# An attention-and-MLP kernel with a written-out order: raw weights over a second queue, half copies by compute engines, and a new account of PSUM tiles

## The chip, the cores and the metric

One core of one Trainium2 chip runs the whole program. The metric is the device time of one execution in microseconds (us). The engines are named as the profile names them: PE (TensorE; PEld is its weight load), DVE (VectorE), ACT (ScalarE), POOL (GpSimd) and SP (SyncE, which here only issues DMAs).

## The reference

```python
q_bits = (einsum('bhsd,dk->bhsk', q, proj) > 0)         # 6 bits for each row of q, the same for k
mask   = q_bucket[:, :, :, None] == k_bucket[:, :, None, :]
scores = where(mask, (1/8) * q @ k.T, -1e9)             # B, H, S, D = 4, 8, 768, 64
attn   = softmax(scores)                                # over 768 keys
x      = (attn @ v) transposed to (3072 tokens, 512)
out    = (relu(x @ w_in) ** 2) @ w_out                  # 512 -> 2048 -> 512, float32
```

## The kernel before, in words

**Stages.** There are 32 pairs of batch and head. A *unit* is 128 queries of one pair against all 768 keys; there are 192 units, worked in *visits* of six (two heads, half of the sequence). When all heads of one half of a batch are done, `moe(n, b, half)` takes these 384 tokens through the two weight matrices; there are eight such blocks.

**A unit** (`unit`): PE makes the scores in PSUM as `pS` (a masked stack `L`,`M` and the stack `A`,`Q`); DVE moves them to `e` with a running maximum; ACT takes the exponential with its row sum in `sums`; DVE or POOL makes `rv` and DVE its reciprocal. In the first four visits, 24 units, POOL divides `e` by its sum, PE transposes it through `pT`, and ACT copies `pT` to `aT`. In later units ACT and DVE split `e` into two float16 halves `hl`, which DMAs transpose into `aT`. `av` multiplies by the values (`pA`) and leaves `xx` as a high and a low half.

**Preparing a pair** (`prep`): DMAs bring `R`; ACT and DVE split it into `A` and `L`; five copies of half stacks (64 partitions each) fill `Q`, `A`, `L` and `M`: `Q<-A`, `Q<-L`, `A<-A`, `L<-M`, `M<-Q`. Before, all five are DMAs on SP.

**Weights** (`fetch`, `split`): 32 pieces of raw weights come in as `raw` (0.5 MB each, three buffers, tag `hl`). A piece then takes `top` on ACT, `f` on DVE, the high half on ACT and the low half on DVE or POOL.

**A block** (`moe`): 16 steps of `pm` (12 matmuls of 384 columns with `win`) and `po` (9 matmuls of 512 columns with `wo`: three tiles of 128 tokens, in three banks of one PSUM tile). ACT takes the relu and the squares, DVE the low half `g`. When the 16th step is done, the three parts of `po` are copied to `o` and sent out. The second half of the last block waits for `verify`, which grades the inputs for the fast path.

**The order.** Instructions are first recorded (`Program.add`), with their dependencies by region. `forward` and `backward` then plan them over five engines with fixed prices; where an operation has several ways, the plan chooses the engine. `emit` writes the instructions in the planned order, and each engine works through its own in that order. The plan only orders: on the chip each instruction waits for semaphores that are set by whole tiles, whatever the plan assumed. A wait in the middle of an engine's order so holds all that stands behind it.

In the profile nearly every instruction has line L427 (a loop in `emit`), matmuls of `matmuls` L424, so groups are told apart by tile names. The program holds a second, general version behind a branch on `flag`; it was not taken, and counts below are of the first alone.

Of the kernel before, what the change touches and what calls it, by code (L numbers as in the profile page):

```python
# [13 lines left out]
F32 = mybir.dt.float32  # L14
# [24 lines left out]
    True: dict(xx=12, hl=3, f=3, e=4, aT=3, g=2, A=8, Q=8, L=8, M=8, R=2, VV=5),  # L39
# [24 lines left out]
RUN = 18  # L64
CONSTS_BY, WIDE = ("sp", "sp", "sp"), 1
# [16 lines left out]
TRANSPOSES = 165  # L82
# [47 lines left out]
class Program:  # L130
# [24 lines left out]
    @staticmethod  # L155
    def region(view):
        ap, rec = view.ap, view.rec
        size = lambda dims: 1 + sum(st * (n - 1) for st, n in dims)
        if rec.kind == "dram":
            return 0, 1, ap.offset, ap.offset + size(ap.ap), 0, 0, 0  # L160
        p0, f0 = divmod(ap.offset, rec.row)
        if rec.kind == "psum":
            return 0, 1, f0 // 512, 1 + (f0 % rec.row + size(ap.ap[1:]) - 1) // 512, 0, 0, 0

        (step, n), inner = ap.ap[1], size(ap.ap[2:])
        block = (step, f0 % step, f0 % step + inner) if n > 1 and f0 % step + inner <= step else (0, 0, 0)
        return (p0, p0 + ap.ap[0][1], f0, f0 + size(ap.ap[1:])) + block

    def add(self, *ways):
# [10 lines left out]
        for rec, w, (p0, p1, f0, f1, fs, g0, g1) in used:  # L180
            if rec.before is not None:
                deps |= rec.before.ops
            for j, w2, (a0, a1, b0, b1, bs, c0, c1) in rec.accesses:
                if (w or w2 or rec.kind == "psum") and a0 < p1 and p0 < a1 and b0 < f1 and f0 < b1 and not (fs and fs == bs and (c1 <= g0 or g1 <= c0)):
                    deps.add(j)
# [9 lines left out]
    def cost(key, name, args, kw):  # L195
# [3 lines left out]
        if name == "matmuls":  # L199

            side = {32: 4, 64: 2}.get(size(args[0][0][1]), 1)
            t = sum(size(a[2]) * column.get(a[2].dtype, 1 / 2.4) + 7 for a, _ in args) / side
            return t, t
# [8 lines left out]
        if name.startswith("dma"):  # L212
# [3 lines left out]
            return busy, b / (TRANSPOSES if name == "dma_start_transpose" else 314)  # L216
# [4 lines left out]
        else:  # L221
            fast = name in ("tensor_copy", "tensor_scalar") and "psum" not in kinds[:2]
            both = len(args) > 3 and isinstance(args[3], View) and args[3].shape[-1] == 1
            t = 67 + 100 * ("accum_out" in kw) + n / (1.92 if fast else 0.96) + 62 * (ptr and (fast or name == "scalar_tensor_tensor")) + 100 * both
# [10 lines left out]
    def port(key, name, args, kw):  # L235
# [7 lines left out]
        return inside and (len(ins) == 2 or name in ("tensor_copy", "tensor_scalar"))  # L243
# [74 lines left out]
    def forward(self, prio, near):  # L318
# [8 lines left out]
        out, dma, dge, held, kind = [], 0.0, 0.0, 0.0, None  # L327
# [11 lines left out]
        while True:  # L339
# [44 lines left out]
            if o.name.startswith("dma"):  # L384
                dge = max(dge, t) + busy if k != "pool" else dge
                busy = dge - t if k != "pool" else busy
                dma = max(dma, t + busy + (650 if k != "pool" else 450))
                if o.name == "dma_start_transpose":
                    o.busy = busy = dma + 467 - t
                dma += done  # L390
                done = dma + 910 - t
# [57 lines left out]
def run(ctx: ExitStack, tc, kq, v, proj2, w_in, w_out, consts, out, flag):  # L449
# [56 lines left out]
    if fast:  # L506
# [8 lines left out]
        codes = sb([P, 4 * P], BF16, "codes")  # L515
# [32 lines left out]
    def fetch(src):  # L548

        raw = sb([P, 512, 2], U32, "raw", tag="hl")  # L550
        send(raw.rearrange("p n t -> p (n t)").bitcast(U16)[:, 0:2047], src.bitcast(U16)[:, 1:2048])
# [79 lines left out]
    def prep(b, hp):  # L631
# [12 lines left out]
        for odd, R in enumerate(Rs):  # L644
# [5 lines left out]
            send(f32(Q[T]), f32(A[U]))  # L650
            send(f32(Q[U]), f32(L[U]))
            send(f32(A[U]), f32(A[T]))
# [6 lines left out]
            send(f32(L[U]), f32(M[T]))  # L659
            send(f32(M[T]), f32(Q[T]))  # L660
# [58 lines left out]
    def values(b, hp, plain):  # L719
# [3 lines left out]
        if fast:  # L723
            vscales[b] = VS, None
            RV = sb([P, 2, KC, D], F32, "V", tag="VV" if plain else "R")
            send(RV, v[b, hp])
# [80 lines left out]
    def moe(n, b, half):  # L807
# [6 lines left out]
        for f in range(NF + 1):  # L814
# [23 lines left out]
            if f > 0:  # L838
# [4 lines left out]
                if first:  # L843
                    po = ps([P, 3, DM], F32, "po")
                for t in range(3):
# [3 lines left out]
                    pe.matmul(po[:, t], gh, wo[:, 0, m], start=first, stop=False)  # L849
                    pe.matmul(po[:, t], gh, wo[:, 1, m], start=False, stop=False)  # L850
                    pe.matmul(po[:, t], gl, wo[:, 0, m], start=False, stop=last)
# [6 lines left out]
                for t in range(3):  # L858
                    r0 = b * S + half * HS + t * P
                    if grouped and last:  # L860
                        if m == 3:
                            move(acc[:, t], po[:, t], back)
                        else:
                            dve.scalar_tensor_tensor(acc[:, t], po[:, t], back, acc[:, t], ALU.mult, ALU.add)
# [168 lines left out]
```

## Time and profile before

| what | before |
|---|---|
| median of 3 runs (lowest to highest) | 832.73 us (830.81 to 833.39) |
| profiled execution: time, span | 834.86 us, 833.1 us |
| mean granted TensorE clock | 0.994 |
| PE, DVE, ACT, POOL busy | 794.3, 605.2, 656.6, 72.7 us |
| DMA | 145.93 MB in 299521 packets; SP's queue 77.2% of 16 engines' span, others 0.6% |

The page lists busy time by engine. The views used below are those of the waits (who sat idle, and what ended it), of windows (busy time in a stretch), of the timeline (instructions in order of time, with the idle time before them in brackets) and of groups by form (a mean duration for each kind of instruction). Instructions of one engine overlap a little, so that durations add up to more than busy time.

### The profile page before, as it was taken

The numbers are of one execution on the slowest core, as the hardware profiler recorded it, in microseconds if no ns is written. First come the engines' busy times: TensorE is split into PE (matmuls) and PEld (weight loads), VectorE is DVE, ScalarE is ACT, GpSimd is POOL, SyncE is SP. The second block draws the span as 40 slices with busy tenths as digits, with TensorE's granted clock in tenths as the row PEclk, the third lists the DMA queues.
The fourth block names the chain that finished last, engine by engine and source line by source line (L and its number), as shares of the span: only waits on it lengthen the run. The fifth ranks groups of instructions, "written<-read, shape, count | busy, mean of one in ns | idle before, by whom it ended". The sixth has DMA issues, their size and how long they took to land. (4 is left out here: it accounts for less than half of the span.)

```text
span 833.1 us, 14383 instructions
## 1 busy us (share of the span) xinstructions
PE 794.3 (95%) x5001; PEld 430.0 (52%) x5001; DVE 605.2 (73%) x1200; ACT 656.6 (79%) x1238; POOL 72.7 (9%) x175
## 2 busy tenths in 40 slices
PE   7797799999999999999999999999999999999996
PEld 4354355555555554555555545555555554555553
DVE  6888989998999888898879755888889433611110
ACT  5898999998888989888898856888988997334443
POOL 1255200100000010000000000000002000000000
PEclk9999999999999999999999999999999999999999
DMA  8985979999999999999989866988975889501001
GB/s 258 270 223 181 292 188 179 214 176 195 183 202 196 195 188 213 192 181 219 194 188 186 212 165 140 181 143 148 146 133 99 239 290 304 212 1 39 1 1 42
DMA packets 299521, 145.93 MB, mean 175 GB/s; under 512 B 268752, under 2 KB 279344, under 8 KB 299440
## 3 DMA queue, kind: packets, MB, share of 16 engines
q1 hardware_dynamic: 299440, 144.93, 77.2%
q8 instruction: 41, 0.67, 0.3%
q14 instruction: 40, 0.33, 0.1%
HBM read 56.80 MB, written 6.29 MB: 76 GB/s over the span
## 5 line engine op out<-in xcount | busy, mean ns | idle before, releaser
L427 PE MATMUL po<-wo,g 128*128 128x512 f16 x1152 | 296.9, 379 | 5.7 <-ACT o L427 5.7
L427 PE MATMUL pm<-xx,win 128*128 128x384 f16 x1536 | 297.7, 326 | 4.4 <-ACT g L427 2.8
L427 PEld LDWEIGHTS <-win 128*128 128x128 f16 x1536 | 149.9, 98 | 116.6 <-issue 8.0
L427 DVE TENSOR_SCALAR_CACHE_REDUCE e<-pS 128x768 f32<-128x768 f32 x192 | 182.7, 953 | 21.9 <-PE pS L427 17.7
L427 ACT ACTIVATE e<-e,maxes 128x768 f32<-128x768 f32 x192 | 178.2, 929 | 20.7 <-DVE e L427 19.2
L427 DVE SCALAR_TENSOR_TENSOR hl<-e,rv,hl 128x768 f16<-128x768 f32 x168 | 171.0, 1019 | 18.8 <-ACT hl L427 17.8
L427 PEld LDWEIGHTS <-g 128*128 128x128 f16 x1152 | 111.9, 98 | 124.8 <-issue 9.1
L427 ACT ACTIVATE hl<-e,rv 128x768 f16<-128x768 f32 x168 | 154.6, 923 | 6.0 <-DMA aT<-hl 5.2
L427 DVE SCALAR_TENSOR_TENSOR g<-g,g 128x384 f16<-128x384 f32 x121 | 66.9, 553 | 111.8 <-ACT g L427 111.4
L427 ACT ACTIVATE g<-g 128x384 f32<-128x384 f32 (+1 forms) x251 | 129.4, 517 | 6.6 <-PE po L427 2.7
L427 ACT ACTIVATE g<-pm 128x384 f32<-128x384 f32 x127 | 61.2, 482 | 90.3 <-PE pm L427 90.0
L427 PE MATMUL pS<-A,Q 128*128 128x384 f16 x372 | 93.1, 330 | 4.1 <-DVE e L427 2.6
L427 PE MATMUL pS<-L,M 128*128 128x384 f16 x372 | 91.8, 327 | 0.8 <-DMA M<-Q 0.8
L424 PE MATMUL pA<-aT,VV 128*64 128x384 f16 x1008 | 87.2, 327 | 0.0
L427 POOL TENSOR_SCALAR rv<-sums 128x1 f32<-128x1 f32 x136 | 36.8, 271 | 541.7 <-ACT e L427 400.2
L424 PEld LDWEIGHTS <-VV 128*64 128x64 f16 x1008 | 54.7, 110 | 32.9 <-issue 10.0
L427 PEld LDWEIGHTS <-Q 128*128 128x128 f16 x372 | 34.2, 98 | 43.1 <-issue 16.2
L427 DVE TENSOR_SCALAR M<-pc,masks 128x384 f16<-128x384 f32 x64 | 43.0, 672 | 15.4 <-PE pc L427 15.2
L427 PEld LDWEIGHTS <-M 128*128 128x128 f16 x372 | 36.3, 98 | 25.1 <-DMA M<-Q 1.2
L427 ACT ACTIVATION_READ_ACCUMULATOR e<-e,maxes 128x1 f32 x192 | 36.6, 191 | 0.0
L427 DVE SCALAR_TENSOR_TENSOR L<-R,A 128x768 f16<-128x768 f32 x32 | 30.4, 950 | 7.7 <-ACT A L427 7.5
L427 PE MATMUL pT<-unit_f,e 128*128 128x128 f32 x144 | 23.8, 293 | 10.5 <-ACT aT L427 7.7
(82 smaller groups left out, 517.4 us busy)
## 6 DMA issues: line engine op xcount, KB each, us to landing
R<-kq SPq DMA_DIRECT2D x32, 384.0 KB, 3.8
X<-kq SPq DMA_DIRECT2D x32, 384.0 KB, 4.1
raw<-w_in SPq DMA_DIRECT2D x16, 511.8 KB, 5.6
raw<-w_out SPq DMA_DIRECT2D x16, 511.8 KB, 4.9
V<-vp SPq DMA_DIRECT2D x20, 384.0 KB, 5.1
out<-o SPq DMA_DIRECT2D x24, 256.0 KB, 2.7
X<-vp SPq DMA_DIRECT2D x16, 384.0 KB, 4.4
Q<-L SPq DMA_DIRECT2D x32, 96.0 KB, 2.9
```

The costliest lines, as they stand in the source:

```text
L424: ins = q.engine.matmul(*map(real, args), **kw).ins
L427: ins = getattr(q.engine, o.name)(*map(real, o.args), **{k: real(x) for k, x in o.kw.items()}).ins
```

## The change: what it does

1. **Raw weights.** From the fourth on (29 of 32), POOL issues the DMA of `raw` and not SP.
2. **Half copies.** In batch 0 the five half copies may be done by SP, POOL or DVE. The plan gives 21 of the 40 to DVE, 8 to POOL, and leaves 11 as DMAs on SP.
3. **Buffers.** `R` has three buffers for two, `VV` four for five; `codes` shares the buffers of `g32`.
4. **The planner's account.** DMAs get other prices, two rings and a limit of 3000 ns on what is queued ahead; a ninth DMA of SP waits for the eighth before it; a few prices of DVE and PE change. PSUM tiles are now whole tiles to the planner, and no longer single banks; two readers of one no longer exclude each other.
5. **The last block.** Its three `po` parts lie in a `pS` tile (two of them) and a `pA` tile. In every block the second of the three is copied out by DVE.

```diff
-    True: dict(xx=12, hl=3, f=3, e=4, aT=3, g=2, A=8, Q=8, L=8, M=8, R=2, VV=5),
+    True: dict(xx=12, hl=3, f=3, e=4, aT=3, g=2, A=8, Q=8, L=8, M=8, R=3, VV=4),
...
+LANES = 8
-TRANSPOSES = 165
+TRANSPOSES, INSIDE, LOADING = 165, 230, 325
+SETUP, LANDING = 100, 1350
+RAW_BY, V_BY = ("pool",), ("sp",)
+HALVES, HALVES_TO = (("sp", "pool", "dve"),) * 5, 1
+AT_MOST, RAW_FROM = 3000, 3
...
         if rec.kind == "psum":
-            return 0, 1, f0 // 512, 1 + (f0 % rec.row + size(ap.ap[1:]) - 1) // 512, 0, 0, 0
+            return 0, 1, 0, 1, 0, 0, 0
...
-                if (w or w2 or rec.kind == "psum") and a0 < p1 and ...
+                if (w or w2) and a0 < p1 and ...
...
+            if way[1].startswith("dma") and rings[int(k == "pool")] > t + AT_MOST:
+                heapq.heappush(later[k], (rings[int(k == "pool")] - AT_MOST, i))
+                continue
...
+                if k != "pool":
+                    lanes.append(t + done)
+                    if len(lanes) >= LANES:
+                        busy = max(busy, lanes[-LANES] + 60 - t)
...
-        codes = sb([P, 4 * P], BF16, "codes")
+        codes = sb([P, 4 * P], BF16, "codes", 2, tag="g32")
...
-        send(raw...[:, 0:2047], src.bitcast(U16)[:, 1:2048])
+        pr.add(*[(getattr(pr, x), "dma_start", (raw...[:, 0:2047], src.bitcast(U16)[:, 1:2048]), {}) for x in (RAW_BY if turn[0] >= RAW_FROM else ("sp",))])
...
-            send(f32(Q[T]), f32(A[U]))
+            by = lambda n: tuple(getattr(pr, x) for x in (HALVES[n] if fast and b < HALVES_TO else ("sp",)))
+            move(f32(Q[T]), f32(A[U]), 1.0, by(0))
...
                 if first:
-                    po = ps([P, 3, DM], F32, "po")
+                    if fast and n == 2 * B - 1:
+                        po = ps([P, 2, 512], F32, "pS"), ps([P, 512], F32, "pA")
+                        po = [po[0][:, 0], po[0][:, 1], po[1]]
+                    else:
+                        po = ps([P, 3, DM], F32, "po")
+                        po = [po[:, t] for t in range(3)]
...
-                        move(o, po[:, t], back)
+                        move(o, po[t], back, (dve,) if fast and t == 1 else (act, dve, pool))
```

PE's last instructions before the branch on `flag`, first of the kernel before; a bracket names the engine whose semaphore the instruction waits for, beside its order.

```order
L427 MATMUL po<-wo,g 128x512 [waits Activation_49]
L427 LDWEIGHTS g
L427 MATMUL po<-wo,g 128x512
L427 LDWEIGHTS g
L427 MATMUL po<-wo,g 128x512
L427 LDWEIGHTS g
L427 MATMUL po<-wo,g 128x512 [waits Activation_49]
L427 LDWEIGHTS g
L427 MATMUL po<-wo,g 128x512
L443 TENSOR_LOAD flag [waits DVE_49]
```

The same place in the changed kernel:

```order
L444 MATMUL pA<-wo,g 128x512
L444 LDWEIGHTS g
L444 MATMUL pS<-wo,g 128x512
L444 LDWEIGHTS g
L444 MATMUL pA<-wo,g 128x512
L444 LDWEIGHTS g
L444 MATMUL pA<-wo,g 128x512
L460 TENSOR_LOAD flag [waits DVE_49]
```

The two waits for ACT inside the last nine matmuls are gone. In the whole order 14 matmuls that write `po` wait for ACT before: 6 open a block, 8 stand inside its last step. Now 5 open a block with such a wait (for ACT or DVE), none stands inside, and one of the last block waits for PE itself.

ACT's order around the first relu of the first block (`g<-pm`), of the kernel before; `xx<-pA` is the fourth of its kind, on which the first `pm` depends.

```order
L427 ACTIVATE wo<-f 128x512
L427 ACTIVATE e,sums<-e,maxes 128x768
L427 ACTIVATE top_87<-raw 128x512
L427 ACTIVATE win<-f 128x512 x2
L427 ACTIVATE xx<-pA 128x384
```

And in the changed kernel:

```order
L444 ACTIVATE wo<-f 128x512
L444 ACTIVATE e,sums<-e,maxes 128x768
L444 ACTIVATE top_86<-raw 128x512
L444 ACTIVATE e,sums<-e,maxes 128x768
L444 ACTIVATE top_83<-raw 128x512
L444 ACTIVATE wo<-f 128x512
L444 ACTIVATE bits<-pd,masks 128x384
L444 ACTIVATE wo<-f 128x512
L444 ACTIVATE xx<-pA 128x384
```

Up to this `xx` ACT now has 13 instructions more: one each of `A`, `VV`, `bits` and `e`, two each of `aT`, `top` and `win`, three of `wo`. No kind has fewer.

POOL's order from its first instruction after the constants, of the kernel before:

```order
L427 TENSOR_SCALAR rv<-sums 128x1
L427 TENSOR_SCALAR e<-e,rv 128x768
L427 TENSOR_SCALAR rv<-sums 128x1
L427 TENSOR_SCALAR e<-e,rv 128x768
L427 TENSOR_SCALAR rv<-sums 128x1
```

And now:

```order
L444 TENSOR_SCALAR Q<-A 64x768
L444 TENSOR_TENSOR L<-R,A 128x768
L444 TENSOR_SCALAR rv<-sums 128x1
L444 DMA raw<-w_in 128x2047
L444 TENSOR_SCALAR e<-e,rv 128x768
L444 TENSOR_SCALAR rv<-sums 128x1
L444 DMA raw<-w_out 128x2047
L444 TENSOR_SCALAR e<-e,rv 128x768
L444 TENSOR_TENSOR win<-f,win 128x512
L444 DMA raw<-w_out 128x2047
```

Between POOL's divisions now stand DMAs of raw weights, half copies, and parts of the splits. Up to the 24th division there are 23 DMAs, 8 half copies, 3 `L`, 7 low halves of weights (4 before) and 15 `rv` (19 before).

More of the change, by code (lines that the diff above doesn't have):

```diff
@@ L215, in cost @@
             busy = 1040 if key == "pool" else (650 if inside else 475) + 50 * (key == "act")
-            return busy, b / (TRANSPOSES if name == "dma_start_transpose" else 314)
+            return busy, SETUP + b / (TRANSPOSES if name == "dma_start_transpose" else INSIDE if inside else LOADING)
         if key == "act":
@@ L223, in cost @@
             both = len(args) > 3 and isinstance(args[3], View) and args[3].shape[-1] == 1
-            t = 67 + 100 * ("accum_out" in kw) + n / (1.92 if fast else 0.96) + 62 * (ptr and (fast or name == "scalar_tensor_tensor")) + 100 * both
+            t = 67 + 100 * ("accum_out" in kw) + n / (3.84 if fast and all(mybir.dt.size(x.dtype) == 2 for x in args[:2]) else 1.92 if fast else 0.96) + 62 * (ptr and (fast or name == "scalar_tensor_tensor")) + 100 * both
         return t, t
@@ L242, in port @@
             return any(x.rec.kind == "sb" for x in args[1:] if isinstance(x, View) and len(x.shape) > 1 and x.shape[-1] > 1)
-        return inside and (len(ins) == 2 or name in ("tensor_copy", "tensor_scalar"))
+        return inside and name in ("tensor_copy", "tensor_scalar")
     def order(self):
@@ L386, in forward @@
                 busy = dge - t if k != "pool" else busy
-                dma = max(dma, t + busy + (650 if k != "pool" else 450))
+                ring = int(k == "pool")
+                dma = max(rings[ring], t + busy + (650 if k != "pool" else 450))
                 if o.name == "dma_start_transpose":
                     o.busy = busy = dma + 467 - t
-                dma += done
-                done = dma + 910 - t
+                shared = min(done, max(0.0, rings[1 - ring] - dma))
+                rings[1 - ring] += shared
+                dma = rings[ring] = dma + done + shared
+                done = dma + LANDING - t
+                if k != "pool":
+                    lanes.append(t + done)
+                    if len(lanes) >= LANES:
+                        busy = max(busy, lanes[-LANES] + 60 - t)
             free[k], o.end = t + busy, t + done
@@ L848, in moe @@
                     pr.rank, pr.mark = RANK_PE, pace()
-                    pe.matmul(po[:, t], gh, wo[:, 0, m], start=first, stop=False)
-                    pe.matmul(po[:, t], gh, wo[:, 1, m], start=False, stop=False)
-                    pe.matmul(po[:, t], gl, wo[:, 0, m], start=False, stop=last)
+                    pe.matmul(po[t], gh, wo[:, 0, m], start=first, stop=False)
+                    pe.matmul(po[t], gh, wo[:, 1, m], start=False, stop=False)
+                    pe.matmul(po[t], gl, wo[:, 0, m], start=False, stop=last)
                     pr.mark = None
```

22 lines of the change are left out of this document (12 added, 10 removed).

## The prediction

> **What bounds the kernel now.** I read the page first, then busy time by window, then who waited for whom, then the timeline at the two places that these point to. From the page:
>
> ```profile
> span 833.1 us, 14383 instructions
> PE 794.3 (95%) x5001; PEld 430.0 (52%) x5001; DVE 605.2 (73%) x1200; ACT 656.6 (79%) x1238; POOL 72.7 (9%) x175
> ```
>
> PE is nearly full, POOL nearly empty. A share over the whole span hides two stages, so here are windows cut at the first exponential (14.8), at the last step before the first `pm` (97.2, 97.7), and at the last matmul (827):
>
> ```profile
> core 0: us, PE busy (x) PEld busy (x) DVE busy (x) ACT busy (x) POOL busy (x), PEclk, DMA share, GB/s
> 0.00:14.80 14.80, 11.36 (x85) 7.01 (x85) 8.00 (x26) 6.41 (x10) 0.21 (x4) 1.00 0.79 250
> 14.80:97.20 82.40, 63.29 (x401) 36.32 (x400) 71.09 (x150) 73.70 (x152) 35.89 (x49) 0.96 0.83 241
> ...
> 97.70:827.00 729.30, 719.65 (x4517) 386.65 (x4516) 525.58 (x1026) 575.37 (x1076) 36.65 (x122) 1.00 0.77 167
> ```
>
> In the long stage after 97.7 PE idles 729.3 - 719.65 = 9.65 us in all: it is the bound, and only what shortens PE's own waits there is worth anything. In the opening PE has 74.65 busy of 97.2 (idle fill among it) and can't do more, since no tokens are ready for a block. There ACT (80.1 busy) and DVE (79.1) are the fullest, neither full. The opening ends when ACT copies the fourth `xx`:
>
> ```profile
> 97.17 0.47 ACT L427 ACTIVATE xx<-pA 128x384 f16<-128x384 f32 x1
> ...
> 97.70 0.32 PE L427 MATMUL pm<-xx,win 128*128 128x384 f16 x1 [1.04 <-ACT xx L427]
> ```
>
> So the time is the end of the opening, plus 729.3 us of PE's work, plus 6.1 us behind the last matmul. PE's waits over the whole run:
>
> ```profile
> PE pT L427 <- ACT aT L427: 7.7, 8, 2.2
> ...
> PE po L427 <- ACT o L427: 5.7, 8, 0.9
> ```
>
> The first lies in the opening (only there is a `pT`). The second is 5.7 of the 9.65 us.
>
> **Term 1: the waits of `po` for ACT.** The timeline at the end shows two of the eight:
>
> ```profile
> 821.67 2.54 PE L427 MATMUL po<-wo,g 128*128 128x512 f16 x11
> ...
> 824.25 0.60 ACT L427 ACTIVATE o<-po 128x512 f32<-128x512 f32 x1 [1.64 <-PE po L427]
> ...
> 824.90 0.81 PE L427 MATMUL po<-wo,g 128*128 128x512 f16 x3 [0.69 <-ACT o L427]
> ...
> 825.74 0.60 ACT L427 ACTIVATE o<-po 128x512 f32<-128x512 f32 x1 [0.90 <-PE po L427]
> 826.39 0.59 PE L427 MATMUL po<-wo,g 128*128 128x512 f16 x2 [0.69 <-ACT o L427]
> ```
>
> ACT copies the first part of `po` while the other two parts are still to be written, and PE stops until the copy is done, although the parts are in different banks. To the planner of before that was free, since it counted banks; the chip waited for the tile. Counting tiles, the new plan has all nine matmuls ahead of the first copy, and its order shows none of the eight waits. A wait costs more than its 0.69 idle: three matmuls take 0.81, and with a mean of 379 ns (page) for one that is (0.81 - 0.38) / 2 = 0.215 between starts, so 0.16 of the matmul ahead would have been overlapped. 5.7 + 8 x 0.16 = **7.0 us less**, all on the path, since PE bounds there. What is late next: a block's first `po` must now wait for three copies. Four matmuls of 384 columns take 0.65 in the chain of waits:
>
> ```profile
> 624.76 0.65 PE pS L427 x4
> ```
>
> Where that first `po` waits, the order puts at least 12 such matmuls in between, 1.95 us, against two copies of 0.60 on ACT beside one on DVE; a few tenths may come back at two or three blocks. At the very end the last copy follows the last matmul as before, so the 6.1 us stay.
>
> **Term 2: the opening.** The order has 13 ACT instructions more ahead of the `xx` that ends it, none fewer. Their prices, from the groups by form between 0 and 97 us:
>
> ```profile
> L427 ACT ACTIVATE e<-e,maxes 128x768 f32<-128x768 f32 x26 | 24.3, 936 | 0.8 <-DVE e L427 0.7
> L427 ACT ACTIVATE aT<-pT 128x384 f32<-128x384 f32 x46 | 20.7, 484 | 2.6 <-PE pT L427 2.4
> L427 ACT ACTIVATE top<-raw 128x512 f16<-128x512 bf16 x22 | 17.2, 783 | 3.9 <-DMA raw<-w_out 2.0 <-DMA raw<-w_in 1.5
> L427 DVE SCALAR_TENSOR_TENSOR f<-raw,top 128x512 uint32<-128x512 uint32 x22 | 15.3, 698 | 0.9 <-ACT top L427 0.9
> L427 ACT ACTIVATE win<-f 128x512 f16<-128x512 f32 x13 | 8.0, 619 | 0.3 <-DVE f L427 0.3
> L427 DVE SCALAR_TENSOR_TENSOR L<-R,A 128x768 f16<-128x768 f32 x8 | 7.6, 950 | 4.1 <-ACT A L427 4.1
> L427 ACT ACTIVATE A<-R 128x768 f16<-128x768 f32 x7 | 5.9, 841 | 4.6 <-DMA R<-kq 4.6
> L427 ACT ACTIVATE wo<-f 128x512 f16<-128x512 f32 x8 | 5.0, 624 | 0.0
> L427 ACT ACTIVATE bits<-pd,masks 128x384 bf16<-128x384 f32 x4 | 2.3, 580 | 0.8 <-PE pc L427 0.6 <-PE pd L424 0.2
> L427 DVE TENSOR_SCALAR codes<-sgn_f 128x128 bf16<-128x128 f32 x4 | 0.7, 224 | 1.4 <-DMA sgn_f<-consts 1.4
> L427 DVE TENSOR_SCALAR A<-R 128x768 f16<-128x768 f32 x1 | 0.5, 541 | 0.0
> ```
>
> One `e` 0.94, one `A` 0.84, one `VV` of the same size and so 0.84, two `aT` 0.97, one `bits` 0.58, two `top` 1.57, two `win` 1.24, three `wo` 1.87: 8.85 us. Instructions overlap by about 0.1 (a `top` of 0.77 begins at 15.72 and the next `e` at 16.36):
>
> ```profile
> 14.79 0.94 ACT L427 ACTIVATE e<-e,maxes 128x768 f32<-128x768 f32 x1
> ...
> 15.72 0.77 ACT L427 ACTIVATE top<-raw 128x512 f16<-128x512 bf16 x1
> 16.36 0.91 ACT L427 ACTIVATE e<-e,maxes 128x768 f32<-128x768 f32 x1
> ```
>
> That leaves 7.5 us, and ACT 80.1 + 7.5 = 87.6 us of work ahead of the first block. DVE fares alike: three `L` fewer (-2.9), five `f` more (+3.5), three `top` and two low halves at about `f`'s 0.7 (+3.5), nine small `rv` and reciprocals at no more than `codes` (+2.0), four copies gone at 0.54 (-2.2), and 21 half copies. No row shows a half copy; it lies between `codes` (0.22) and the full copy of `A` (0.54), nearer the latter, whose 768 columns it has: 0.4, so 8.4 in all (4.7 to 11.4). Net +12.4, and with an overlap of 0.1 for each of 33 instructions some +9: 88 us, just as full as ACT.
>
> What pays for it is ACT's idle time, 17.1 us in the opening: 14.8 - 6.4 = 8.4 ahead of the first `e`, and 82.4 - 73.7 = 8.7 behind it. The first part mostly stays: constants, `K`, `G`, `pd`, `pc`, `MK` and `pS` follow one another as before. The order puts both `K`, `G` and `pj` ahead of the first `R`, worth two issues of SP (0.43 each, below): I put the first `e` at 13.9. Of the 6.4 us that ACT did ahead of it, two `top`, a `win` and a `bits` (2.7) now stand behind it, so 87.6 - 3.7 = 83.9 remain: **no earlier than 13.9 + 83.9 = 97.8** can the fourth `xx` begin, about where it is today. A gain in the opening would need less work than the order shows. How much of the 8.7 us of later idling goes, then? By name:
>
> ```profile
> POOL rv L427 <- ACT e L427: 40.4, 17, 15.5
> ...
> PEld pT L427 <- POOL e L427: 8.6, 8, 2.5
> ...
> ACT A L427 <- DMA R<-kq: 4.6, 2, 3.0
> ...
> ACT top L427 <- DMA raw<-w_out: 2.0, 2, 1.6
> ...
> ACT top L427 <- DMA raw<-w_in: 1.5, 3, 0.6
> ```
>
> The 3.0 for `R` is ahead of the first `e`; 1.6 of it and 3.5 for `raw` are behind, 5.1 in all. SP's own waits say why:
>
> ```profile
> SPq L427 <- DVE f L427: 12.5, 9, 6.7
> ```
>
> SP holds all that stands behind a `raw` until a buffer is free, `R` and half copies among it. With `raw` on POOL, three buffers of `R`, and half copies that need no landing, I take the 5.1 as gone and 3.6 as staying. Against that POOL must now issue 23 DMAs ahead of its 24th division, each behind the same wait for `f`, and the divisions queue behind them; PE already waits on these (8.6 above). I put 0.5 us net there. Fourth `xx` at 97.8 + 3.6 + 0.5 = 101.9 against 97.2: **4.7 us more**. PE has meanwhile done four more `pS`, a `pc` and a group of `pd` (0.65 for four matmuls, so about **1.2 us** taken from later).
>
> The 11 half copies left on SP, the four `VV` and the shared `codes` I cost at nothing: SP's queue is emptier, and `VV` is fed by `V` loads of which only two were waited for.
>
> **Term 3: the rest of the order.** Three more splits of `wo` and five more `f` done early relieve ACT and DVE behind 97.7, but PE hardly waited there: at most 1 us. New waits from a new order of 4517 matmuls may cost as much. Taken as 0, with 2 us either way.
>
> **The sum.** -7.0 + 4.7 - 1.2 = -3.5. Against the profiled execution (834.86 us, whose span is 833.1 with 1.8 around it) that is 831.4; that execution stands 2.1 above the median of 832.73, which the prediction refers to: **829.2 us**, 0.4% less. Bounds: with no idle time of ACT behind the first `e`, and 1 us from term 3, 832.7 - 7.0 + 0.6 - 1.2 - 1 = 824.1; with the first `e` two microseconds earlier still, and 2 us of term 3, 821. With all 8.7 of idling still there and POOL in the way for 4 more, the fourth `xx` is at 110.5: -7 + 13.3 - 1.2 = +5.1, or 837.8.
>
> **Rivals.**
> *A: the opening costs nothing.* Fourth `xx` at 98 or before: 832.7 - 7.0 - 1.2 + 0.8 = 825.3 or less. For it: idle time by lateness of DMAs is just what the change touches. Against: 87.6 us of work in ACT's order.
> *B: POOL becomes the bound of the opening* (slower). Up to the 24th division its order holds 24 divisions, 23 DMAs, 8 half copies, 3 `L`, 7 low halves and 15 `rv`:
>
> ```profile
> L427 POOL TENSOR_SCALAR rv<-sums 128x1 f32<-128x1 f32 x21 | 6.7, 320 | 40.7 <-ACT e L427 40.4
> L427 POOL TENSOR_TENSOR win<-f,win 128x512 f16<-128x512 f32 x3 | 3.5, 1173 | 4.1 <-ACT win L427 4.0
> ```
>
> ```profile
> L427 POOL TENSOR_SCALAR e<-e,rv x24: 907/909/1468, 17.0 to 89.6; 128x768 f32<-128x768 f32 x24
> ```
>
> ```profile
> 6.51 1.29 SPq L427 DMA_DIRECT2D raw<-w_in  x3
> ```
>
> The first two rows are groups by form, the third is the division with its least, median and longest time and first and last start, the fourth SP's issue. 24 x 0.91 + 23 DMAs + 8 half copies at a division's 0.91 + 3 x 1.76 (1.173, and half as many columns again) + 7 x 1.17 + 15 x 0.32. A DMA on POOL has no row: SP issues one in 0.43, POOL's longest instruction here takes 1.76; I take 1.0, nearer the other POOL rows (10 to 40 us for 23). That is 70 us, behind a start at about 16, and 97.2 - 89.6 = 7.6 more from the last division to `xx`: 94 if POOL never waits. If it waits over 15 us, for buffers (12.5 on SP today) or for divisors, the fourth `xx` is past 109 and the 7.0 us are spent: 835 to 840.
>
> The Trainium skill has a rule for this (SBUF — State Buffer, "SBUF: two separate sides"): while DVE runs an instruction in a two-port mode, GpSimd can't write descriptors; in the next section, on a bandwidth pool, a DMA of 620 ns beside such a copy took 3100. No run here shows it yet; by that figure an estimate is 2.5 us for each DMA that meets one of 24 copies of some 0.4 us in 97, about one in ten, 6 us of POOL's time in all, and the sum would be 831 to 835 for it. Its chance lies within B's.
>
> *C: the waits of `po` come back* as waits of the next block's first `po`, or for other copies: half of term 1 lost, 832.7, no change that can be measured.
>
> **Chances.** Forecast 0.56, A 0.18, B 0.16, C 0.10. About 0.3%, 2.5 us, is what a measurement of this kernel can tell from no change. Of the forecast's own cases (fourth `xx` from 98 to 106, the earlier half likelier) seven in ten are faster than 830.2, which needs it by 102.9, and nearly all others within the bound. Faster: 0.56 x 0.7 + 0.18 + 0.03 of C = 0.60; same 0.16 + 0.07 = 0.23; slower 0.17. The range of 821 to 837 leaves out the far end of A and the worse half of B.
>
> **What the profile will show.** Term 1: no row of `po` waiting for ACT `o` of 5 us, and PE idle under 6 us between the first `pm` and the last matmul. Term 2: the first `pm` between 99 and 105, ACT over 86 us busy ahead of it, SP's waits for `f` near nothing, POOL over 65 us busy. B would show POOL with hardly any wait for ACT `e`, and PE's weight loads of `pT` waiting for POOL well over 15 us. A first `pm` before 97 makes term 2 wrong, eight new waits in the blocks term 1.

## The result: 5.3% slower, and the profile after

| | before | after |
|---|---|---|
| median (lowest to highest) | 832.75 us (830.81 to 833.39) | 876.79 us (874.99 to 878.12) |
| ratio, 95% interval | | 1.0531 [1.0504, 1.0559] |
| first `pm` (end of the opening) | 97.7 us | 131.8 us |
| from there to the first `pm` of the third block | 216.7 us | 229.9 us |
| from there to the start of the last matmul | 512.2 us | 505.1 us |

The median of before now has a fourth run. The last three rows are read off the starts of PE's instructions. Of the 40.2 us between the last matmuls (826.6 and 866.8), 34.1 were lost in the opening and 13.2 in the two blocks behind it; 7.1 were won in the other six. The page of the changed kernel begins:

```profile
span 874.1 us, 14381 instructions
...
PE 814.7 (93%) x5018; PEld 438.4 (50%) x5018; DVE 624.8 (71%) x1226; ACT 658.5 (75%) x1231; POOL 110.4 (13%) x214
...
q0 software_dynamic: 2320, 15.20, 5.9%
```

PE's busy time grew by 20, although it has nearly the same instructions; the windows, cut like those of before, tell where: 17.5 of the 20 are in the opening (busy time of PE, PEld, DVE, ACT and POOL, granted clock, share of the DMA engines, GB/s):

```profile
0.00:131.30 131.30, 92.16 (x514) 50.77 (x515) 100.57 (x208) 89.54 (x175) 68.40 (x88) 0.86 0.58 177
131.80:867.00 735.20, 722.29 (x4504) 387.62 (x4503) 523.31 (x1018) 567.91 (x1055) 42.03 (x126) 0.99 0.76 162
```

In the opening PE ran at a granted clock of 0.86 where before had 0.96 to 1.00. ACT's work is 89.5, close to the 87.6 forecast. DVE's is 100.6, where 88 were forecast, and no engine fills the 131.3 us: something else sets the pace. What lies behind the opening, split at the start of the third block, of before and then of the changed kernel:

```profile
97.70:314.40 216.70, 213.89 (x1408) 115.86 (x1408) 196.92 (x397) 196.34 (x360) 16.30 (x56) 1.00 0.96 195
314.40:826.60 512.20, 505.38 (x3108) 270.79 (x3108) 328.67 (x630) 379.03 (x717) 20.35 (x66) 1.00 0.69 155
```

```profile
131.80:361.70 229.90, 217.95 (x1395) 116.91 (x1395) 190.70 (x380) 191.02 (x345) 21.52 (x61) 0.97 0.87 170
361.70:866.80 505.10, 504.14 (x3110) 270.71 (x3108) 332.42 (x638) 376.89 (x711) 20.52 (x65) 1.00 0.70 158
```

In the first two blocks PE idles 12.0 us where before has 2.8; in the other six it idles 1.0 for 6.8. From the view of the waits:

```profile
PEld pT L444 <- POOL e L444: 28.9, 14, 4.7
...
PE pT L444 <- POOL e L444: 20.6, 13, 4.1
...
PE po L444 <- ACT o L444: 0.3, 1, 0.3
```

PE now waits for POOL's divisions; its old waits for `o` are nearly gone (5.7 before). POOL's timeline (start, duration, in brackets the idle time before and what ended it) shows what the divisions wait for:

```profile
41.54 0.59 POOL L444 DMA_DIRECT2D raw<-w_out  x1 [3.04 <-ACT aT L444]
...
46.06 0.59 POOL L444 DMA_DIRECT2D raw<-w_in  x1 [1.73 <-ACT top L444]
...
50.85 0.59 POOL L444 DMA_DIRECT2D raw<-w_in  x1 [1.11 <-DVE Q L444]
51.49 3.02 POOL L444 TENSOR_SCALAR e<-e,rv 128x768 f32<-128x768 f32 x2
54.92 0.59 POOL L444 DMA_DIRECT2D raw<-w_in  x1 [0.40 <-DVE M L444]
...
59.65 0.65 POOL L444 DMA_DIRECT2D raw<-w_in  x1 [0.26 <-DVE M L444]
```

A DMA takes POOL some 0.6 us, yet two of them are never closer than 4.01 us in the whole run (29 of them). The brackets name DVE and ACT instructions of the moment; most of those have nothing to do with the transfer. The trace also has each transfer's landing: the five DMAs shown start 0.31 us after the landing of the one before (41.23, 45.75, 50.54, 54.61 and 59.34 us). Of the 28 that follow another, 26 start 0.30 or 0.31 us behind its landing, and none starts while another is in flight. If the pieces are split in the order of their loads, the `f` that frees the buffer had ended 2.2 to 6.5 us before each of the five. A name that changes from row to row while the distance stays is a sign that the true releaser isn't in the list. The page's list of DMA issues (count, size, median us from issue to landing) has nearly the same number:

```profile
raw<-w_out POOLq DMA_DIRECT2D x16, 511.8 KB, 3.9
...
raw<-w_in POOLq DMA_DIRECT2D x13, 511.8 KB, 3.9
```

So it is one transfer at a time; what limits it to one is what the first group of experiments asks.

### The profile page after: what moved, and what is told of

Same layout as the page of the kernel before. It is cut to its first block, busy times and chain, and to the rows that moved or that the text cites. A ratio compares the mean times of both kernels' runs of the same rounds, so it can differ in the third digit from the quotient of the medians.

```text
span 874.1 us, 14381 instructions
## 1 busy us (share of the span) xinstructions
PE 814.7 (93%) x5018; PEld 438.4 (50%) x5018; DVE 624.8 (71%) x1226; ACT 658.5 (75%) x1231; POOL 110.4 (13%) x214
## 4 chain that ended last, share of the span: by engine, by line
PE 79%; ACT 2%; issue 2%; DVE 1%; DMA 1%; POOL 0%; POOLq 0%; DVEq 0%; ACTq 0%
PE pm L444 27%; PE po L444 24%; PE pS L444 14%; PE pA L441 10%; PE pA L444 1%; DMA raw<-w_out 1%; PE pd L441 1%; PE pc L444 1%; ACT hl L444 1%; DVE hl L444 0%; ACT o L444 0%; ACT g L444 0%; PE pt L444 0%; DVE e L444 0%; ACT e L444 0%
## 5 line engine op out<-in xcount | busy, mean ns | idle before, releaser
L444 PE MATMUL pm<-xx,win 128*128 128x384 f16 x1536 | 314.6, 328 | 4.2 <-ACT g L444 2.9
L444 PE MATMUL po<-wo,g 128*128 128x512 f16 x1008 | 285.0, 381 | 5.5 <-ACT g L444 5.2
L444 ACT ACTIVATE g<-g 128x384 f16<-128x384 f32 (+1 forms) x249 | 128.3, 517 | 7.8 <-PE po L444 3.5
L444 PE MATMUL pS<-A,Q 128*128 128x384 f16 x372 | 97.0, 337 | 8.2 <-DVE e L444 8.1
L444 PE MATMUL pS<-L,M 128*128 128x384 f16 x372 | 97.5, 335 | 1.8 <-DVE rv L444 1.8
L444 POOL TENSOR_SCALAR rv<-sums 128x1 f32<-128x1 f32 x127 | 33.3, 262 | 480.4 <-ACT e L444 331.1
L444 PE MATMUL pT<-unit_f,e 128*128 128x128 f32 x144 | 29.2, 337 | 25.0 <-POOL e L444 20.6
L444 PEld LDWEIGHTS pT<-unit_f,e 128*128 128x128 f32 x144 | 20.7, 172 | 38.2 <-POOL e L444 28.9
L444 DVE RECIPROCAL rv<-rv 128x1 f32<-128x1 f32 x192 | 30.0, 158 | 10.3 <-POOL rv L444 8.3
```

Source lines behind the costliest of these rows:

```text
L444: ins = getattr(q.engine, o.name)(*map(real, o.args), **{k: real(x) for k, x in o.kw.items()}).ins
```

## The experiments

Theories are numbered anew in each group, as the expectations state them. A `before` on the same chips had medians of 831.5 to 833.3.

### GpSimd's queue

The program sets `dynamic_dma_scratch_size=256`, the room for the DMAs of GpSimd, in both kernels; before, none went there. Two kernels change only this number, so that their order is that of the changed kernel.

```diff
-    nc = bacc.Bacc("TRN2", ..., dynamic_dma_scratch_size=256)
+    nc = bacc.Bacc("TRN2", ..., dynamic_dma_scratch_size=512)    # and 1024
```

> The changed kernel with twice the scratch for DMAs that POOL issues (512 for 256 bytes a partition); the planned order is the same to the last row. Theory 1 (the scratch holds one such transfer, so that POOL stands at each raw DMA until the one before has landed, at least 4.0 us after its issue): two are in flight, the least distance between raw DMAs falls from 4.0 us to about 2, the first pm comes at 98 to 108 instead of 131.8, and the time falls from 877 to 828 to 850 us. Theory 2 (a DMA costs POOL some 4 us whatever is in flight): 877 us, distance 4.0. Theory 3 (the raw buffers, which wait for DVE's f, set the pace): 877 us as well.

> The changed kernel with four times the scratch (1024 bytes a partition), again in the same order. Theory 1: the wait is gone altogether, since three raw buffers allow no more than three in flight; distances down to 1 to 2 us, first pm at 96 to 104, time 822 to 836 us, no slower than with 512. Theories 2 and 3: 877 us.

Measured: 851.55 us with 512, 1.0227 [1.0190, 1.0264], and 849.44 us with 1024, 1.0205 [1.0169, 1.0242]. With either the smallest distance of two DMAs falls from 4.01 to 1.36 us, and up to two transfers are in flight when another is issued. With 1024 the weight loads' wait for POOL falls from 28.9 to 6.6:

```profile
PEld pT L444 <- POOL e L444: 6.6, 8, 1.3
```

The same instructions in the same order are 25 and 27 us faster: this is the larger part of the loss, and it is shown; the 877 us of theories 2 and 3 are out. But both times and both openings (118.1 and 116.5) are later than theory 1 had them, so that some 17 us have another cause. Does the queue cost as much without the rest of the change? The kernel before with raw weights on POOL, and nothing else:

```diff
-        send(raw..., src...)
+        (pool if turn[0] >= 3 else sp).dma_start(raw..., src...)
```

> The kernel before with one edit: raw weights from the fourth on issued by GpSimd, whose queue has the same 256. Theory 1: GpSimd's DMAs stand 4 us apart and hold the divisions; 23 of them ahead of the 24th division at 4.0 are 92 us and 24 divisions 22 more, so the fourth xx comes at 115 to 130 and the time is 848 to 868. If the queue only hurts together with the half copies and the new account: 830 to 840.

Measured: 880.26 us, 1.0568 [1.0538, 1.0597], beyond the expected range. The groups by form of its opening (0 to 133.4 us; busy time and mean of one, then the idle time of POOL before them) and its waits:

```profile
L427 POOL DMA_DIRECT2D raw<-w_in x13 | 7.6, 586 | 39.7 <-DVE f L427 11.5 <-issue 9.4 <-DVE xx L427 7.1
L427 POOL DMA_DIRECT2D raw<-w_out x11 | 6.3, 572 | 33.2 <-issue 10.0 <-ACT e L427 7.8 <-DVE MK L427 4.9
```

```profile
PEld pT L427 <- POOL e L427: 33.1, 15, 8.4
```

13.9 us of issuing, and 72.9 us in which POOL stood ahead of them; not all of that is lost, since before POOL idled 61.6 of the opening's 97.7 us. Of the 28 DMAs that follow another, 25 start 0.30 to 0.32 us after its landing. This edit alone makes the kernel before as slow as all edits together. Then single instructions by themselves, with the same 256; six DMAs of 0.5 MB go to six free buffers:

```diff
+        for n in range(6):
+            go("pool", load(n))         # and divisions, half copies and f, alone and side by side
```

> Leaves out the whole computation: it only repeats single instructions of the opening on DVE and GpSimd, alone and side by side, with GpSimd's queue of 256 as in the changed kernel, and writes zeros. Alone: f 0.65 to 0.70 us, a half copy on DVE 0.2 to 0.35, a division 0.91, a half copy on GpSimd 0.8 to 1.1, a DMA on GpSimd 0.6. Theory 1 (a queue of 256 has room for one transfer): six DMAs in a row, with six free buffers and nothing beside them, stand 3.7 to 4.1 us apart. If the buffers or the divisions were what held them, they would stand about 1 us apart. Theory 4 (DVE and GpSimd keep each other waiting): 30 half copies on DVE beside eight divisions take the sum of both and not the longer of the two (some 8 + 8 us, where side by side would be 8), and f beside divisions is stretched likewise to 0.9 or more; copies out of PSUM beside divisions are not stretched. If theory 4 is wrong, every mean stays within 10% of that alone.

```profile
32.97 0.73 POOL L139 DMA_DIRECT2D raw<-w_out  x1
37.29 0.55 POOL L139 DMA_DIRECT2D raw<-w_out  x1 [3.59 <-issue]
41.50 0.54 POOL L139 DMA_DIRECT2D raw<-w_out  x1 [3.66 <-issue]
45.57 0.54 POOL L139 DMA_DIRECT2D raw<-w_out  x1 [3.53 <-issue]
```

4.1 to 4.3 us apart (a little more than expected) with nothing to wait for but the transfer ahead, and here the trace calls it "issue". The Trainium skill (DMA: Bandwidth & Descriptors, "Anatomy of one DMA — SWDGE (gpsimd) path") fits a transfer with a fixed 2.0 us and its bytes at 436 GB/s, which makes an estimate of 3.2 us for this size. Here the six took 3.8 to 4.0 us from issue to landing.

### DVE beside GpSimd

The same kernel's timeline goes on, with sums of a series in the second column. Alone (first four rows), then pairs of series that start together:

```profile
6.83 6.10 DVE L130 SCALAR_TENSOR_TENSOR f<-src,top 128x512 uint32<-128x512 uint32 x10
...
13.03 3.87 DVE L133 TENSOR_SCALAR Q<-A 64x768 f16<-64x768 f16 x10
...
17.33 7.07 POOL L136 TENSOR_SCALAR e<-e,rv 128x768 f32<-128x768 f32 x8
...
25.11 7.19 POOL L133 TENSOR_SCALAR M<-L 64x768 f16<-64x768 f16 x8
...
58.30 14.09 DVE L130 SCALAR_TENSOR_TENSOR f<-src,top 128x512 uint32<-128x512 uint32 x16
...
59.00 14.15 POOL L136 TENSOR_SCALAR e<-e,rv 128x768 f32<-128x768 f32 x8
...
73.53 16.33 DVE L133 TENSOR_SCALAR Q<-A 64x768 f16<-64x768 f16 x30
...
73.92 7.93 POOL L136 TENSOR_SCALAR e<-e,rv 128x768 f32<-128x768 f32 x8
...
104.80 23.46 DVE L133 TENSOR_SCALAR Q<-A 64x768 f16<-64x768 f16 x60
```

```profile
89.97 14.74 DVE L130 SCALAR_TENSOR_TENSOR f<-src,top 128x512 uint32<-128x512 uint32 x16
...
90.78 9.77 POOL L133 TENSOR_SCALAR M<-L 64x768 f16<-64x768 f16 x8
...
156.78 9.42 DVE L185 TENSOR_SCALAR A<-pc 128x384 f16<-128x384 f32 x16
...
157.11 7.07 POOL L136 TENSOR_SCALAR e<-e,rv 128x768 f32<-128x768 f32 x8
```

Sixteen `f` would take 9.8 us alone and eight divisions 7.1; side by side both take 14.1, where the sum is 16.8. Beside eight half copies of POOL (7.2 alone) the `f` take 14.7 and the half copies 9.8. Thirty half copies on DVE beside eight divisions take 16.3 instead of 11.6, the divisions 7.9. Copies out of PSUM leave the divisions at their 7.07. Sixty half copies beside six DMAs take 0.391 each, as alone (0.387), and the DMAs' issues keep 0.54 to 0.71. So of the 7.1 us in which both engines could work, DVE loses 4.3 with `f` and 4.7 with half copies: here the two engines' work on SBUF held each other up for more than half of that time, though not for all of it. The issuing of DMAs was not held up. The Trainium skill has a rule for the first (SBUF — State Buffer, "Who interferes with whom": an instruction with two SBUF inputs, or a copy in a two-port mode, and a GpSimd instruction that reads SBUF block each other). For `f`, which has two inputs, the run agrees, apart from the 2.7 us that did overlap; in which mode the half copies ran, no row says. The stretched DMA that the prediction weighed is not seen: 3.8 to 4.1 us to landing beside the half copies, 3.8 to 4.0 alone.

Does this explain what is left with the wider queue? First, half copies stay free to choose, raw weights return to SP:

```diff
-RAW_BY, V_BY = ("pool",), ("sp",)
+RAW_BY, V_BY = ("sp",), ("sp",)
```

> The changed kernel with all raw weights on SP again (planned anew, everything else kept). Theory 1 and theory 2 alike: the opening gets back what POOL's DMAs took, first pm at 95 to 103, 822 to 833 us. Theory 4 (the half copies on POOL and DVE, or the new prices, spoil the opening): first pm after 110 and more than 845 us.

Measured: 848.35 us, 1.0213 [1.0170, 1.0256]. The opening ends at 105.2, 26.6 us earlier, but only 28.4 of 44 us come back, which fits neither theory. Then three kernels on the one with 1024. The change had also altered `port()`, by which the plan keeps instructions of DVE and POOL apart; two SBUF inputs no longer count. The first kernel undoes that, the second the half copies, the third both:

```diff
-        return inside and name in ("tensor_copy", "tensor_scalar")
+        return inside and (len(ins) == 2 or name in ("tensor_copy", "tensor_scalar"))
```
```diff
-HALVES, HALVES_TO = (("sp", "pool", "dve"),) * 5, 1
+HALVES, HALVES_TO = (("sp", "pool", "dve"),) * 5, 0
```

> The changed kernel with room for more transfers on GpSimd's own queue (849.4 us in the earlier run) and, on top, the planner's old rule that keeps every DVE instruction with two SBUF inputs apart from GpSimd's. Left to explain is 849.4 - 832.7 = 16.7 us, with the first pm at 116.5 us where before has 97.7, and DVE busy 105 of those 116. Theory 1 (DVE and GpSimd block each other in the opening, because the new rule no longer keeps the two-input instructions f, L and VV apart from GpSimd's): f falls from 996 towards 700 ns and L from 1383 towards 950, DVE is busy 92 or less ahead of the first pm, which comes at 104 to 108, and the time is 836 to 842. Theory 2 (the half copies on GpSimd and DVE are what costs): 846 to 851. Theory 3 (the new prices and the third R order the work worse): 846 to 851.

> The same kernel with the wider queue, where all half copies of batch 0 go back to SP's DMAs and the new planner's rule stays. Theory 1 (the rule lets DVE and GpSimd block each other): GpSimd still has raw DMAs, e, wo and L, so most stays, 843 to 849. Theory 2 (the half copies cost): they are 20 instructions that now leave GpSimd, DVE; the first pm at 103 to 108 and 836 to 841. Theory 3 (prices, third R): 846 to 851.

> Both edits at once on the kernel with the wider queue: old rule, and half copies by SP. What is left of the change is raw weights on GpSimd, the limit on queued transfers with the new prices, the third R and the PSUM part, which alone gave 828.3. Theory 1 and theory 2 both: the first pm at 95 to 103 and 826 to 835, and whichever of the two kernels beside it comes nearer to this one has the larger part. Theory 3 (prices, third R): 845 to 850 still.

Measured: 856.48 us (1.0285 [1.0248, 1.0321]), 849.80 (1.0221 [1.0188, 1.0253]) and 843.32 (1.0114 [1.0089, 1.0140]). The first is above all three ranges, the last between those of theories 1 and 2 and that of theory 3. The old rule alone does shorten `f` (996 to 750 ns), as theory 1 had it, and yet makes the kernel 7 us slower; these are the groups by form up to the first `pm`, of the kernel with 1024 and of the one with the old rule:

```profile
L444 DVE SCALAR_TENSOR_TENSOR f<-raw,top 128x512 uint32<-128x512 uint32 x27 | 26.7, 996 | 0.8 <-ACT top L444 0.7
```

```profile
L444 DVE SCALAR_TENSOR_TENSOR f<-raw,top 128x512 uint32<-128x512 uint32 x26 | 19.3, 750 | 1.0 <-ACT top L444 0.7
```

So the theory that the rule costs the rest falls. That what is kept apart must wait instead, and that the amount of work on the two engines counts, fits the numbers but was not tested by itself. Under the old rule, undoing the half copies gains 13.2 us; there they raise POOL's busy time ahead of the first `pm` from 53.9 to 66.4 and DVE's from 88.4 to 100.7, and the first `pm` from 111.5 to 118.8. Under the new rule undoing them gains nothing (849.80 for 849.44), the time that theory 3 had. None of the three comes near 832.7; from the first `pm` to the third block they take 220.5 to 230.5 us, where before takes 216.7.

### The order behind the opening

With raw weights and half copies on SP and the old rule, little is left that could make the opening later. Only prices, limit, buffers and the PSUM part are left (the edits to `RAW_BY`, `HALVES_TO` and `port()` above, at 256):

> No raw weights on GpSimd, old rule, half copies by SP: of the change stay the new DMA and DVE prices, the limit on queued transfers, the third R and the PSUM part. Theory 1 and theory 2: nothing costly is left, 824 to 831 with the first pm at 91 to 98, near the 828.3 of the PSUM part alone. Theory 3 (prices, third R): clearly above, 836 to 846 (the kernel with raw on SP but the rest of the change was 848.4).

Measured: 843.87 us, 1.0126 [1.0106, 1.0147], as theory 3 had it; the first `pm` at 97.4, but 230.5 us from there to the third block (216.7 before). Windows of before, then of this kernel:

```profile
150.00:300.00 150.00, 149.31 (x1017) 81.77 (x1016) 136.53 (x277) 132.98 (x242) 8.54 (x37) 1.00 1.00 194
300.00:330.00 30.00, 28.85 (x178) 15.56 (x177) 25.46 (x53) 27.82 (x54) 2.58 (x7) 1.00 1.00 218
```

```profile
150.00:300.00 150.00, 146.18 (x973) 79.60 (x971) 126.38 (x260) 126.54 (x228) 10.62 (x35) 1.00 0.91 180
300.00:330.00 30.00, 22.65 (x143) 10.88 (x143) 23.99 (x48) 20.57 (x36) 1.33 (x7) 0.83 0.90 168
```

From 150 to 300 us DVE does 10 us less, and the DMA engines have 0.91 of their time for 1.00: the attention of batch 1 falls behind. By 300 us all 384 `pm` of the first two blocks and 60 transposes of `hl` have started, before 372 and 64. So PE then has no tokens for a block and works through the late units one by one. The waits between 98 and 330 us have it too (0.3 in this row before):

```profile
PE pS L444 <- DVE e L444: 10.1, 9, 2.2
```

Four kernels each undo one group of edits in it:

```diff
-R=3, VV=4                                                        # two R
+R=2, VV=5
-AT_MOST, RAW_FROM = 3000, 3                                      # no limit
+AT_MOST, RAW_FROM = 10**9, 3
-TRANSPOSES, INSIDE, LOADING = 165, 230, 325                      # old DMA account, with no limit
+TRANSPOSES, INSIDE, LOADING = 165, 314, 314
-SETUP, LANDING = 100, 1350
+SETUP, LANDING = 0, 910
-LANES = 8
+LANES = 10**6
-                t *= 0.5 if args[0][0][2].dtype == F32 else 0.7  # old engine prices, with DVE's 3.84 as 1.92
```

> From the kernel with raw weights on SP, half copies on SP and the planner's old rule for two inputs (843.9 us): its opening ends at 97.4 us as before the change (97.7), but from the first pm to the start of the third block PE idles 37.4 us where before has 22.9, most of it at 300 to 325 us. Four edits remain in it; each of four kernels undoes one. This one: two buffers of R and five of VV again. Theory 3a (the four VV hold back the second batch's values and with them its attention): the third block starts at 314 to 320 and the time is 830 to 836. Theories 3b (the limit), 3c (the DMA prices), 3d (prices of PE and DVE): 841 to 847.

> The same kernel of 843.9 us without the limit of 3000 ns on queued transfers. Theory 3b (the limit holds SP's copies and transposes back in the plan, so that the attention of the second batch comes late): the third block starts at 314 to 320 where it was at 327.8, and the time is 830 to 836. Theories 3a, 3c, 3d: 841 to 847.

> The same kernel of 843.9 us with the DMA account of before: old speeds, no setup, 910 ns to landing, no wait for the eighth DMA ahead, no limit. Theory 3c (the prices make the plan believe that transposes come later than they do, and so it orders other work ahead): 828 to 836, and better than without the limit alone. Theory 3b: the same time as the kernel without the limit, within 2 us. Theories 3a, 3d: 841 to 847.

> The same kernel of 843.9 us with the old prices of PE (attention by plain V at full price) and DVE (two-byte copies at the old speed). Theory 3d (the plan takes the plain A times V products for half of what they cost, and so falls behind): the third block at 314 to 320, the time 830 to 836. Theories 3a to 3c: 841 to 847.

Measured, in this order: 842.80 us (1.0128 [1.0095, 1.0161]), 847.65 (1.0182 [1.0147, 1.0217]), 830.65 (0.9973 [0.9954, 0.9992]) and 838.84 (1.0076 [1.0045, 1.0107]). The DMA account is it: 13.2 us, with 212.0 us to the third block. The old engine prices gained 5.0, less than theory 3d has and more than the others allow; two `R` changed nothing that can be told. Windows of the kernel with the old account:

```profile
150.00:300.00 150.00, 150.00 (x1021) 82.04 (x1019) 136.48 (x284) 133.54 (x244) 8.15 (x32) 1.00 1.01 195
300.00:330.00 30.00, 29.20 (x186) 15.42 (x186) 27.51 (x57) 27.61 (x51) 2.24 (x9) 1.00 0.98 197
```

The account takes no time on the chip, and between these two kernels only seven instructions of ACT, DVE and POOL change their engine; what differs is the order. In PE's order 134 matmuls `pS<-A,Q` stand ahead of the 289th `pm` with the new account, 140 with the old: attention comes later. Which line of it? Undoing the limit alone made the kernel 3.8 us slower. The lanes alone:

```diff
-LANES = 8
+LANES = 10**6
```

> The kernel of 843.9 us (raw and half copies on SP, old rule) without the wait of a ninth DMA of SP for the eighth before it; prices and limit of the DMAs stay new. Undoing the whole DMA account gave 830.7, the limit alone 847.7. If the eight lanes are what makes the plan lag: 829 to 835, third block at 310 to 318. If the prices (slower copies, 1350 ns to landing): 841 to 847.

Measured: 846.83 us, 1.0155 [1.0125, 1.0185]; not the lanes. That leaves the prices of setup, speed and landing, or several lines together; this was not divided further. Does the account cost the same beside raw weights on POOL? The kernel with 1024, and the old account as above (the plan's second ring stays):

> The changed kernel with room for more transfers on GpSimd (849.4 us) and the DMA account of before, all else as changed: raw on GpSimd, half copies by any engine, new rule, three R. If the causes add up, what is left over 832.7 is 849.4 - 13.2 = 836, with PE idling some 12 us between the first and the third block's start less than the 26.2 of the kernel it comes from; DVE beside GpSimd in the opening stays, and the first pm at 112 to 117. If the account matters only with raw on SP: 846 to 851.

Measured: 845.52 us, 1.0154 [1.0124, 1.0184]. From the first `pm` to the third block it takes 213.2 where 218.5 stood, but the time falls by 3.9 only, not by 13: the causes don't add up. It is still 12.8 us over before; the opening ends 16.6 us later (114.3 for 97.7).

### What is worth keeping

The PSUM part by itself, on the kernel before (the account by whole tiles, the last block's `po` in `pS` and `pA`, the second copy of `po` by DVE):

```diff
-            return 0, 1, f0 // 512, ...
+            return 0, 1, 0, 1, 0, 0, 0
...
-                        move(o, po[:, t], back)
+                        move(o, po[t], back, (dve,) if fast and t == 1 else (act, dve, pool))
```

> The kernel before with part 4's account of PSUM as whole tiles and part 5 (last block in pS and pA, second copy by DVE) alone. By term 1 of the prediction the eight waits of po for ACT go (5.7 us idle, 7.0 us in all): 825 to 827 us against 832.7. The rival: they come back as waits at the next block or the new order loses them elsewhere: 831 to 834 us.

Measured: 828.28 us, 0.9960 [0.9941, 0.9978]. The waits of `po` for ACT fall from 5.7 us to 0.5, but the time is above the 825 to 827 that term 1 gives. From the third block on:

```profile
312.10:821.80 509.70, 506.24 (x3114) 270.32 (x3112) 329.91 (x637) 375.58 (x712) 23.80 (x68) 1.00 0.71 155
```

That is 2.5 us less than before, with PE idle for 3.5 us where it was 6.8. The last matmul starts 4.8 us earlier, and 4.4 of these come from an opening that ends at 93.3, of which term 1 says nothing. Last, the kernel of 830.65 us with the edit to `R` and `VV` above, and another with that to the engine prices instead:

> Towards a version that beats both: PSUM by whole tiles, raw and half copies on SP, old rule, old DMA account (830.7 us), and two buffers of R with five of VV. In the kernel with the new account these buffers had their opening end 2 us earlier (95.4 for 97.4) and gained 1.1 us. If that carries over: 827 to 830 with the first pm at 97 to 100. If the third R is worth something once SP is not held back: 831 to 834.

> The same kernel of 830.7 us with three R and the old prices of PE and DVE. In the kernel with the new DMA account the old prices gained 5.0 us, with the third block 2.7 us earlier. If that carries over: 825 to 829. If the old prices only made up for the lag that the new DMA account caused: 829 to 833, the same within what can be told.

Measured: 830.33 us, 0.9976 [0.9957, 0.9995], and 830.74 us, 0.9982 [0.9968, 0.9995]. Buffers and engine prices are worth nothing that can be told once the account is the old one. The PSUM part alone has the lowest time found, though its interval overlaps those of these kernels.

| kernel | us | first `pm` | to the third block | to the last matmul |
|---|---|---|---|---|
| before | 832.75 | 97.7 | 216.7 | 512.2 |
| after | 876.79 | 131.8 | 229.9 | 505.1 |
| after, queue 512 | 851.55 | 118.1 | 219.5 | 505.6 |
| after, queue 1024 | 849.44 | 116.5 | 218.5 | 505.1 |
| ... old rule | 856.48 | 118.8 | 222.1 | 507.4 |
| ... half copies on SP | 849.80 | 102.3 | 230.5 | 505.6 |
| ... both | 843.32 | 111.5 | 220.6 | 507.7 |
| ... old DMA account | 845.52 | 114.3 | 213.2 | 507.3 |
| after, raw on SP | 848.35 | 105.2 | 227.5 | 506.7 |
| ... half copies on SP, old rule | 843.87 | 97.4 | 230.5 | 506.3 |
| ...... no limit | 847.65 | 95.7 | 237.9 | 506.1 |
| ...... old DMA account | 830.65 | 101.5 | 212.0 | 507.8 |
| before, raw on POOL | 880.26 | 133.4 | 228.4 | 508.4 |
| before, PSUM part | 828.28 | 93.3 | 218.8 | 509.7 |

Each median is of all its runs, the other columns, as in the table of the result, are of one profiled execution. A late opening is not wholly lost (the two kernels of 843 differ by 14.1 in it), since work that is done in it is missing behind it; that is an explanation from the counts, not a test.

## Why the prediction was wrong

Forecast were 829.2 us, 821 to 837; measured 876.79.

**The step that failed most: a DMA on POOL at 1.0 us, and "0.5 us net" for POOL in term 2.** No row showed one, so it was bounded by rows of SP's issue and of POOL's compute. Neither end held a wait. With 256 the chip issues in 0.54 to 0.73 and starts no second transfer until the first has landed: 4.0 us and more each. 25 of them stand ahead of the first `pm`. On one path from after to before, the queue is worth 27.4 us of the 44.0. Rival B named the place and the signs (POOL over 65 us busy, here 68.4; weight loads of `pT` waiting over 15 us, here 28.9; POOL's wait for ACT `e` in the opening, 40.4 before, without a row), and had them at 835 to 840, since it was built from the same price. A bound from both sides should have held the case that a DMA stands until it lands: the page of before has 4.9 and 5.6 us from issue to landing for SP's loads of the same size, and these were the nearest rows.

**DVE's 88 us of work in the opening.** Measured 100.6. The count of instructions was right (27 `f`, 21 half copies); the durations were those of a DVE beside a POOL that was half idle. `f` took 882 ns for 698, which is 4.8 us; the half copies on DVE 12.1 us in sum for 8.4, though one alone takes 0.387, as estimated at 0.4; five `L` 6.7 for 4.7. Putting work on an idle engine was taken as free for its neighbour. It wasn't: the single instructions side by side show such stretching, though not how much of it made the opening longer.

**Term 3 at 0, within 2.** The two blocks behind the opening cost 13.2 us. With the wider queue 1.8 of these are left, so that most belonged to the queue here; but without raw weights on POOL the new DMA account alone costs 18.4 in the same place and 13.2 in all. The new prices are in the list of changes, and the prediction never asked what order they make. Of what term 2 cost at nothing, the four `VV` did hold SP for 29.8 us in the opening (2.5 before), yet five again gained only 1.1 and 0.3 us.

**Term 1: the waits right, the 7.0 us not shown.** The waits of `po` went from 5.7 us to 0.3, as forecast, and the last six blocks took 7.1 us less. That this is so near 7.0 is partly luck: the kernel before with raw weights on POOL, which has no PSUM part, also took 3.8 less there, and the PSUM part alone took 2.5 less. In the whole kernel the part alone gained 3.3 us (0.4% [0.2%, 0.6%]), by its profile most of it in the opening. New waits of `po` and `pS` for DVE (1.1 and 0.6 us) stand in the last six blocks of that kernel.

**The forecast's own signs.** The first `pm` at 131.8 and not 99 to 105: wrong. PE idle under 6 us behind it: 735.2 - 722.3 = 12.9, wrong. ACT over 86 busy: 89.5, right. SP's waits for `f`: gone, since the loads now stand in POOL's order.

On the path after, 1024, both undone, raw on SP, old account, before, the 44.0 us divide into 27.4 (queue), 6.1 (half copies and rule together), -0.6 (raw weights on POOL with room), 13.2 (DMA account) and -2.1 (the rest, the PSUM part among it). The -0.6 can't be told from nothing. Another path gives other parts, as the kernels with the rule alone (+7.0) and with the account beside raw on POOL (-3.9) show. Why undoing the half copies gains nothing by itself (849.80 for 849.44) stays open and is only described here: 14.2 us in the opening, given back in the next two blocks and a little behind them.

## What to carry to other kernels

Price a DMA that moves to another engine by what may be in flight on the new queue as well as by its issue, and look at what stands behind it in that engine's order; a constant distance between issues, with a different releaser in every row, was here the sign of a full queue, and the landing of the transfer before settled it. Work that goes to an idle engine isn't free if it holds up a neighbour: measure both beside each other. And a planner's price is an edit of the order; where it moves hardly an instruction to another engine, its cost still has to be looked for, stage by stage.

## What the runs showed of the hardware that was not expected

- GpSimd's DMAs of 0.5 MB came no closer than 4.0 us with `dynamic_dma_scratch_size=256`, most of them 0.31 us after the landing of the one before, and as close as 1.36 with 512 or 1024, in the same order of instructions.
- `f` and the division, side by side, took 14.1 us for 9.8 and 7.1 alone; copies out of PSUM beside divisions left these at 7.07.
- PE's granted clock was lower in some stretches in which PE waited: 0.86 over the changed kernel's opening (PE busy for 70%; before 0.97 at 76%), and 0.83 at 300 to 330 us of the kernel with the late attention, where it was 0.50 from 316.2 to 325: two `pS` matmuls took 0.80 us at 316.2, and 0.48 at 313.5. The busy share alone doesn't set it, since the opening of the kernel of 830.65 us has 0.93 at 81%.
